# Keeping one piece of w3 in its slot between two layers of a decode kernel, with one slot fewer for wq

## The chip, the cores and the metric

The kernel runs on one core of one Trainium2 chip. The metric is device microseconds of one execution, median of three runs. The core has a tensor engine (PE, with its weight loads, PEld), a vector engine (DVE), a scalar engine (ACT), GpSimd (POOL), and a sync engine (SP) that here issues nearly all DMA transfers. All transfers from HBM go through one queue that 16 DMA engines serve, each with a fixed sixteenth of every transfer.

## The reference

One token (a vector of 640 values) goes through two identical layers with shared weights and shared caches. Cut to what matters:

```
W = 4096                                   # the last 4096 cached positions
q = (LN(x) @ wq) as 32 heads of 192        # wq: 640 x 6144
o = softmax(q k^T / sqrt(192)) v           # per head: k, v are 4096 x 192, bf16
x = x + o @ wo                             # wo: 6144 x 640
g = LN(x) @ w1 ; u = LN(x) @ w3            # w1, w3: 640 x 1536
x = x + (silu(g) * u) @ w2                 # w2: 1536 x 640
(the same four steps once more, same weights, same caches)
```

Keys, values and weights are the same in both layers, so what still lies in on-chip memory from layer 0 need not be read again in layer 1.

## The kernel before, in words

All large data lie in one on-chip buffer, `arena`, cut into 32 units ("slots") of 3072 bf16 columns on 128 partitions, 768 KB each. A page of k or v is 6144 columns, two slots. The list `loads` names every transfer of the program in the order of its issue: for each layer the pieces of wq, the pages of k and v, the pieces of wo, then w1, w3 and w2 (the kinds "fa", "fb", ...). `refill()` takes the head of that list, `place()` looks for free slots, and the transfer is issued on SP (L279; L268 for the fixed buffers `wo5` and `keep`); if no slot is free, the list stops there, strictly in order. `done(key)` is written behind the last matmul that reads a piece: it gives the slots back and calls `refill()`. So a transfer's issue on SP waits for the matmuls that read the slot's old contents, and SP's later transfers wait behind it. SP also keeps at most eight transfers under way, so where slots are plenty it issues one whenever the oldest has landed.

Some k heads of layer 0 stay for layer 1: 13 pages (26 slots) remain in the arena, a 14th is moved to PSUM and a spare buffer (`stash`, DVE copies on L288) and copied back in layer 1. At the end of layer 0 only slots 0, 1, 4 and 5 are therefore in turn for wo, w1, w3, w2 and, behind them, layer 1's wq.

Layer 0's FFN (`ffn`) reads w1 and w3 in pieces of one slot: fa and fb (w1, two of five row chunks each), fc (w1's last and w3's first chunk), fd (w3's chunks 1 and 2), fe (w3's chunks 3 and 4); fg and fh are w2, whose last 2240 columns stay in `keep` for both layers. A chunk is 1536 columns, and four matmuls on four column groups of PE compute it. Layer 1 loads w1 as one transfer (fa, 7680 columns), w3 as fb (4608) and fc (3072), and w2 in three parts under the key fd.

Between the layers (`attention`, `q_piece`), layer 1's wq comes as ten one-slot pieces, in the order q0, q12, q24, q36, q48 (first half of the heads), then q6, q18, q30, q42, q54. Six matmuls read each (1.04 us at the clock there); then its slot takes the next load. After the first five, ACT copies the result out and `q_turn` transposes it; q6 and q18 follow, then the first k page (head 8, still in the arena), and q30, q42 and q54 each behind one k page. Each retained k page that is read gives two slots. The first new loads behind wq are halves of k and v pages ("k", 1, 12, half 0), and so on.

At the end of layer 1, `ffn` runs its steps in program order: five chunks of w1 (`g_ps`), `out_residual` (two f32 matmuls that add the residual), then w3 (`u_ps`) with `gate()` (SiLU of g) behind the second w3 chunk, then ACT's copy of u (L588), `turn(1)`, the product on DVE (L590, `htd`), and `last_rows`: 48 matmuls with w2, 14 of them from `keep`. A DVE copy (L617) and a transfer of 1.2 KB (L619) end the kernel. PE's order is fixed by `pin`.

Of the kernel before, what the change touches and what calls it, by code (L numbers as in the profile page):

```python
# [17 lines left out]
NCH = 5  # L18
# [7 lines left out]
PGW = 6144  # L26
# [18 lines left out]
KEEP = 2240  # L45
# [10 lines left out]
def kernel(  # L56
# [39 lines left out]
    onesD, rl, st, nv, rstd, lnv, l = (sc[:, a:b] for a, b in ((0, 1), (1, 3), (3, 5), (7, 8), (5, 6), (6, 7), (6, 8)))  # L96
# [57 lines left out]
    loads = []  # L154
# [4 lines left out]
    w3_v = B_w3.rearrange("(p c) n -> p (c n)", c=NCH)  # L159
    w2_v = B_w2.rearrange("(p f) n -> p (f n)", f=12)  # L160
# [3 lines left out]
    def head(layer, g):  # L164
        return HG * ORDER[layer][g // HG] + g % HG

    def k_head(layer, g):
        return HG * ORDER[1][0] + (0, 1, 2, 3, 6, 4, 5, 7)[g] if layer == 1 and g < HG else head(layer, g)

    def k_first(layer, i):  # L170
        return layer == 0 and H - HB <= i < H
# [12 lines left out]
    def q_pieces(layer):  # L184
        if layer == 0:
            at = (0, 12, 24, 60)
            return [tuple(range(a, b)) for a, b in zip(at, at[1:])]
        return [tuple(range(12 * c + 6 * f, 12 * c + 6 * f + 6)) for f in range(2) for c in range(NCH)]
# [4 lines left out]
    def units_of(width):  # L193
        return -(-width // U)

    for layer in range(2):
        for piece in q_pieces(layer):
            n, at = 512 * len(piece), 512 * piece[0]
            loads.append((("q", layer, piece[0]), units_of(n), [(0, n, wq_r[:, at:at + n])]))
        for i in range(H + LEAD):  # L200
            kinds = (("v", i - LEAD, A_v_cache), ("k", i, A_k_cache))
            for kind, g, cache in kinds[::-1] if k_first(layer, i) else kinds:
                if not 0 <= g < H:
                    continue
                h = k_head(layer, g) if kind == "k" else head(layer, g)
                if kind == "k" and layer == 1 and h in RETAIN:
                    if h == STASH:
                        loads.append((("k", 1, h), 2, []))
                    continue
                src = cache[0, h, S0:SK, :].rearrange("(p t) d -> p (t d)", p=P)  # L210
                if layer == 1 and (kind, h) in SPLIT:
                    for th in range(2):
                        loads.append(((kind, layer, h, th), 1, [(0, U, src[:, U * th:U * th + U])]))
                else:
                    loads.append(((kind, layer, h), 2, [(0, PGW, src)]))
        for key, ranges in wo_units(layer):
            at, parts = 0, []
            for pos, lo, hi in ranges:
                parts.append((at, hi - lo, wo_v[ORDER[layer][pos]][:, lo:hi]))
                at += hi - lo  # L220
            if key:
                loads.append((key, units_of(at), parts))
            else:
                dst = wo5 if at == 2560 else wo4
                if dst is wo5:
                    src = parts[0][2]
                    parts = [(o, n, src[:, o:o + n]) for o, n in tail_cuts(2560)]
                loads.append((None, None if dst is wo5 else LAST, [(dst[:, o:o + n], src) for o, n, src in parts]))
        if layer == 0:
            loads.append((("fa", layer), 1, [(0, 3072, w1_v[:, 0:3072])]))  # L230
            loads.append((("fb", layer), 1, [(0, 3072, w1_v[:, 3072:6144])]))
            loads.append((("fc", layer), 1, [(0, 1536, w1_v[:, 6144:]), (1536, 1536, w3_v[:, 0:1536])]))
            loads.append((("fd", layer), 1, [(0, 3072, w3_v[:, 1536:4608])]))
            loads.append((("fe", layer), 1, [(0, 3072, w3_v[:, 4608:])]))
            loads.append((("fg", layer), 1, [(0, W2A, w2_v[:, 0:W2A])]))
            loads.append((("fh", layer), 1, [(0, 7680 - KEEP - W2A, w2_v[:, W2A:7680 - KEEP])]))
            loads.append((None, None, [(keep[:, o:o + n], w2_v[:, 7680 - KEEP + o:7680 - KEEP + o + n])
                                       for o, n in tail_cuts(KEEP)]))
        else:
            loads.append((("fa", layer), units_of(7680), [(0, 7680, w1_v[:, 0:7680])]))  # L240
            loads.append((("fb", layer), 2, [(0, 4608, w3_v[:, 0:4608])]))
            loads.append((("fc", layer), 1, [(0, 3072, w3_v[:, 4608:])]))
            loads.append((("fd", layer), 2, [(o, n, w2_v[:, o:o + n]) for o, n in ((0, 3200), (3200, 1280), (4480, 3200 - KEEP))]))

    def place(key, n):
        at = [s for s in free if all(s + i in free for i in range(n))]
# [44 lines left out]
    def page(key, width=PGW):  # L291
        return arena[:, home[key][0] * U:home[key][0] * U + width]
# [257 lines left out]
    def ffn(layer, last, spread):  # L550
        g_ps = ps_a.tile([P, 512], F32, tag="a", name="g_ps")
        u_ps = ps_a.tile([P, 512], F32, tag="a", name="u_ps")
        gu = w20.rearrange("p (g n) -> p g n", g=2)
        gt_ps = (m_ps[:, 0:12], g_ps[:, 384:396])

        def turn(gi):
            for k in range(3):
                mm(gt_ps[gi][:, 4 * k:4 * k + 4], lhsT=gu[:, gi, k:384:3], rhs=sel4, start=True, stop=True)

        def gate():  # L560
            pin(nc.scalar.mul(out=gu[:, 0, :], in_=g_ps[:, 0:384], mul=rstd))
            turn(0)
            pin(nc.scalar.activation(out=ex[:], in_=gt_ps[0], func=ACTF.Exp, scale=-1.0))
            pin(nc.vector.tensor_scalar_add(out=ex[:], in0=ex[:], scalar1=1.0))
            pin(nc.vector.reciprocal(out=ex[:], in_=ex[:]))
            pin(nc.vector.tensor_tensor(out=ut[:], in0=gt_ps[0], in1=ex[:], op=ALU.mult))

        if layer == 0:
            steps = ((g_ps, "fa", 0, 2, 0), (g_ps, "fb", 2, 4, 0), (g_ps, "fc", 4, 5, 0),
                     (u_ps, "fc", 0, 1, 1536), (u_ps, "fd", 1, 3, 0), (u_ps, "fe", 3, 5, 0))  # L570
        else:
            steps = ((g_ps, "fa", 0, 5, 0), (u_ps, "fb", 0, 3, 0), (u_ps, "fc", 3, 5, 0))
        for n, (ps, kind, c0, c1, off) in enumerate(steps):
            pg = page((kind, layer), 7680 if (kind, layer) == ("fa", 1) else PGW)
            for c in range(c0, c1):
                for j in range(4):
                    mm(ps[32 * j:32 * j + 32, 0:384], lhsT=xs[:, c, 3:35],
                       rhs=_ap(pg, 0, P, off + 1536 * (c - c0) + 3 * j, [[12, 128], [1, 3]]),
                       start=(c == 0), stop=(c == NCH - 1), tile_position=(0, 32 * j))
                if ps is g_ps and c == 0:  # L580
                    spread()
                if ps is u_ps and c == layer:
                    gate()
            if layer == 0 and all(st[1] != kind for st in steps[n + 1:]):
                done((kind, layer))
            if layer and n == 0:
                out_residual(*last)
        pin(nc.scalar.mul(out=gu[:, 1, :], in_=u_ps[:, 0:384], mul=rstd))  # L588
        turn(1)
        pin(nc.vector.tensor_tensor(out=_ap(htd[:], 0, P, 0, [[1, 3], [3, 4]]),  # L590
                                    in0=gt_ps[1].rearrange("p (k j) -> p k j", k=3),
                                    in1=ut[:].rearrange("p (k j) -> p k j", k=3), op=ALU.mult))
        if layer == 1:
            return last_rows(last[0])
        y_ps = y_open("y2_ps")
        for fcx in range(9):
            j = fcx % 4
            for nh in range(2):
                lo, hi = 640 * fcx + 320 * nh, 640 * fcx + 320 * nh + 320
                cuts = [lo] + [7680 - KEEP] * (lo < 7680 - KEEP < hi) + [hi]  # L600
                for c0, c1 in zip(cuts, cuts[1:]):
                    mm(y_ps[nh][32 * j:32 * j + 1, c0 - lo:c1 - lo], lhsT=htd[:, fcx:fcx + 1], rhs=w2_cols(layer, c0, c1 - c0),
                       start=False, stop=(fcx >= 5 and c1 == hi), tile_position=(0, 32 * j))
            if 640 * fcx < W2A <= 640 * fcx + 640:
                done(("fg", layer))
        done(("fh", layer))
        y_to_residual(y_ps, (keep[:, KEEP - TAIL:], htd, 9))
# [107 lines left out]
```

## Time and profile before

| | |
|---|---|
| runs | 524.82, 525.02, 525.16 us; median 525.02 |
| profiled execution | 524.09 us, of which its instructions span 522.3 us |
| moved from HBM | 219.78 MB, 421 GB/s over the span |
| busy | PE 290.0 us (56%), DVE 261.6 (50%), ACT 81.3 (16%), POOL 22.3 (4%) |
| chain that ended last | DMA 85%, PE 9%, DVE 3%, ACT 1% |

The digit rows of the page cut the span into 40 slices: the DMA row is 9 (90% or more) in every slice but the last. PE and DVE are busy half of the time. A timeline row gives start and duration, the engine and line, the operation with its operands and count, and in brackets the idle time before it with what ended it.

### The profile page before, as it was taken

The numbers are of one execution on the slowest core, as the hardware profiler recorded it, in microseconds if no ns is written. First come the engines' busy times: TensorE is split into PE (matmuls) and PEld (weight loads), VectorE is DVE, ScalarE is ACT, GpSimd is POOL, SyncE is SP. The second block draws the span as 40 slices with busy tenths as digits, with TensorE's granted clock in tenths as the row PEclk, the third lists the DMA queues.
The fourth block names the chain that finished last, engine by engine and source line by source line (L and its number), as shares of the span: only waits on it lengthen the run. The fifth ranks groups of instructions, "written<-read, shape, count | busy, mean of one in ns | idle before, by whom it ended". The sixth has DMA issues, their size and how long they took to land.

```text
span 522.3 us, 5553 instructions
## 1 busy us (share of the span) xinstructions
PE 290.0 (56%) x2163; PEld 107.7 (21%) x2163; DVE 261.6 (50%) x338; ACT 81.3 (16%) x224; POOL 22.3 (4%) x104
## 2 busy tenths in 40 slices
PE   3325755364555645556466786677346655364565
PEld 1101221121212112112112232222112212121132
DVE  0079876556746576763001107532678565565111
ACT  1010211120303021112001013122301220122001
POOL 4010000000000000000000001000000000000100
PEclk9677677777776668666666567889557787778667
DMA  9999999999999999999999999999999999999996
GB/s 377 404 429 431 430 428 429 427 429 429 433 427 432 429 428 431 427 430 429 424 416 415 423 404 427 429 429 429 429 429 432 428 429 429 428 431 427 433 429 263
DMA packets 24081, 220.13 MB, mean 421 GB/s; under 512 B 2808, under 2 KB 3704, under 8 KB 8952
## 3 DMA queue, kind: packets, MB, share of 16 engines
q1 hardware_dynamic: 23912, 219.79, 99.5%
q8 instruction: 17, 0.28, 0.2%
q14 instruction: 8, 0.07, 0.0%
q10 hardware_dynamic: 144, 0.00, 0.0%
HBM read 219.78 MB, written 0.00 MB: 421 GB/s over the span
## 4 chain that ended last, share of the span: by engine, by line
DMA 85%; PE 9%; DVE 3%; ACT 1%; issue 1%; SPq 0%; ACTq 0%; DVEq 0%
DMA arena<-in_A_k_cache_dram 47%; DMA arena<-in_A_v_cache_dram 28%; DMA arena<-in_B_w_dram 5%; PE s_ps L87 4%; DMA arena<-in_A_wo_dram 3%; DMA arena<-in_A_wq_dram 3%; PE o_ps L87 2%; DVE arena L397 2%; PE pss L87 1%; PE q_ps L87 1%; PE y_ps L87 1%; ACT w L472 0%; DVE w L472 0%; SPq L279 0%; ACT ptm L444 0%
## 5 line engine op out<-in xcount | busy, mean ns | idle before, releaser
L87 PE MATMUL s_ps<-arena,wst 128*16 128x512 bf16 (+1 forms) x768 | 143.6, 523 | 146.0 <-DVE arena L397 69.9
L397 DVE STREAM_TRANSPOSE arena<-arena 128x3072 uint32<-128x3072 uint32 (+1 forms) x53 | 168.5, 3189 | 58.6 <-DMA arena<-in_A_k_cache_dram 58.2
L87 PE MATMUL o_ps<-arena,ptm 128*16 128x512 bf16 (+1 forms) x768 | 130.2, 495 | 20.5 <-DMA arena<-in_A_v_cache_dram 20.5
L87 PEld LDWEIGHTS <-wst 128*16 128x16 bf16 (+1 forms) x768 | 46.7, 109 | 233.4 <-issue 208.9
L87 PEld LDWEIGHTS <-ptm 128*16 128x16 bf16 (+1 forms) x776 | 37.9, 105 | 73.4 <-issue 58.3
L428 ACT ACTIVATE lt<-w 32x16 f32<-32x16 f32 x16 | 3.4, 211 | 263.3 <-DVE w L425 263.3
L444 ACT COPY ptm<-w 32x96 bf16<-32x96 bf16 x80 | 25.9, 324 | 48.4 <-PE o_ps L87 34.4
L472 DVE CAST w<-o_ps 32x512 bf16<-32x512 f32 x16 | 11.0, 689 | 40.5 <-ACT w L472 40.3
L87 PE MATMUL q_ps<-arena,xs 128*32 128x512 bf16 x120 | 19.5, 587 | 13.9 <-DMA arena<-in_A_wq_dram 12.8
L87 PE MATMUL pss<-w,sel 96*64 96x192 bf16 x64 | 12.2, 278 | 23.1 <-ACT w L472 15.3
L420 DVE TENSOR_REDUCE lt<-s_ps 64x1 f32<-64x512 f32 x16 | 10.9, 684 | 24.6 <-PE s_ps L87 22.6
L472 ACT CAST w<-o_ps 32x512 bf16<-32x512 f32 x32 | 18.4, 575 | 25.9 <-PE o_ps L87 25.4
L382 POOL COPY wst<-qt_sb 32x24 bf16<-32x24 bf16 x30 | 8.4, 280 | 323.3 <-PE s_ps L87 241.2
L434 DVE STREAM_TRANSPOSE w<-w 64x512 bf16<-64x512 bf16 x16 | 11.3, 705 | 14.7 <-ACT w L431 13.8
L87 PE MATMUL y_ps<-arena,otd 128*1 128x320 bf16 x176 | 14.0, 420 | 7.6 <-DMA arena<-in_A_wo_dram 7.3
L444 DVE COPY ptm<-w 32x96 bf16<-32x96 bf16 x48 | 10.8, 226 | 10.5 <-PE o_ps L87 9.4
L87 PEld LDWEIGHTS <-xs 128*32 128x32 bf16 x200 | 7.6, 111 | 30.3 <-issue 25.8
L382 DVE COPY wst<-qt_sb 32x24 bf16<-32x24 bf16 x4 | 0.8, 212 | 25.8 <-ACT qt_sb L369 25.8
L327 DVE CAST w<-y_ps 128x320 bf16<-128x320 f32 x3 | 1.5, 492 | 23.7 <-PE y_ps L87 23.7
L87 PEld LDWEIGHTS <-sel 96*64 96x64 bf16 x64 | 6.1, 118 | 30.9 <-ACT w L472 16.7
L431 ACT ACTIVATE w<-s_ps,eu 64x512 bf16<-64x512 f32 x16 | 10.9, 682 | 6.0 <-DVE eu L429 6.0
L478 DVE SCALAR_TENSOR_TENSOR w<-pss,sc,cb 64x192 bf16<-64x192 f32 x16 | 6.6, 410 | 9.1 <-PE pss L87 9.1
(86 smaller groups left out, 126.6 us busy)
## 6 DMA issues: line engine op xcount, KB each, us to landing
arena<-in_A_v_cache_dram SPq DMA_DIRECT2D x62, 1536.0 KB, 29.2
arena<-in_A_k_cache_dram SPq DMA_DIRECT2D x47, 1536.0 KB, 29.2
arena<-in_A_wq_dram SPq DMA_DIRECT2D x10, 768.0 KB, 7.4
arena<-in_A_wq_dram SPq DMA_DIRECT2D x1, 4608.0 KB, 19.8
arena<-in_A_k_cache_dram SPq DMA_DIRECT2D x6, 768.0 KB, 9.7
arena<-in_A_wo_dram SPq DMA_DIRECT2D x6, 720.0 KB, 7.8
arena<-in_B_w_dram SPq DMA_DIRECT2D x5, 768.0 KB, 7.7
arena<-in_A_wo_dram SPq DMA_DIRECT2D x2, 1920.0 KB, 30.1
```

The lines of the kernel that those rows point to most:

```text
L87: return pin(nc.tensor.matmul(*a, **k))
L327: pin(nc.vector.tensor_copy(out=y_sb[:, 320:640], in_=y_ps[1][:, 0:320]))
L382: pin((engs[a].copy if engs[a] is nc.scalar else engs[a].tensor_copy)(out=dst, in_=src))
L397: pin(nc.vector.transpose(x.bitcast(U32), x.bitcast(U32)))
L420: pin(nc.vector.reduce_max(out=t0[:, 0:1], in_=s_ps[0:64, :], axis=AX.X))
L428: pin(nc.scalar.mul(out=t0[32:64, 0:KW].rearrange("p (a z) -> p a z", a=4), in_=mb, mul=-SCALE))
L431: pin(nc.scalar.activation(out=e[:], in_=s_ps[0:64, :], func=ACTF.Exp, bias=nbt[:, 0:1], scale=SCALE, accum_out=l[0:64, b % 2:b % 2 + 1]))
L434: pin(nc.vector.transpose(et[:], e[:]))
L444: pin((eng.copy if eng is nc.scalar else eng.tensor_copy)(out=dst, in_=src))
L472: pin(nc.vector.tensor_copy(out=dst, in_=src) if c == 2 else nc.scalar.copy(out=dst, in_=src))
L478: pin(nc.vector.scalar_tensor_tensor(out=om, in0=ot_ps, scalar=rl[0:64, b % 2:b % 2 + 1], in1=mask[0:64].unsqueeze(2).broadcast_to([64, 16 ...
```

## The change

Layer 0's fe (w3's columns 4608 to 7680, the row chunks 3 and 4) is not given back after its use: its slot, number 0, stays occupied until the end. Layer 1 reads those two chunks from it, directly behind w1, and loads only the rest of w3, as 3072 columns (fb) and 1536 columns (fc). The key fc of layer 1 shrinks to half, the three w2 transfers are cut at 3200, 4800 instead of 3200, 4480. The gate comes behind chunk 4, which is now the second one in the order. Start and stop flags of the accumulation follow the new order of chunks. With slot 0 gone, three slots (1, 4 and 5) are in turn for wq between the layers.

```diff
-            loads.append((("fb", layer), 2, [(0, 4608, w3_v[:, 0:4608])]))
-            loads.append((("fc", layer), 1, [(0, 3072, w3_v[:, 4608:])]))
-            loads.append((("fd", layer), 2, [(o, n, w2_v[:, o:o + n]) for o, n in ((0, 3200), (3200, 1280), (4480, 3200 - KEEP))]))
+            loads.append((("fb", layer), 1, [(0, 3072, w3_v[:, 0:3072])]))
+            loads.append((("fc", layer), 1, [(0, 1536, w3_v[:, 3072:4608])]))
+            loads.append((("fd", layer), 2, [(o, n, w2_v[:, o:o + n]) for o, n in ((0, 3200), (3200, 1600), (4800, 2880 - KEEP))]))
...
-            steps = ((g_ps, "fa", 0, 5, 0), (u_ps, "fb", 0, 3, 0), (u_ps, "fc", 3, 5, 0))
+            steps = ((g_ps, "fa", 0, 5, 0), (u_ps, "fe", 3, 5, 0), (u_ps, "fb", 0, 2, 0), (u_ps, "fc", 2, 3, 0))
         for n, (ps, kind, c0, c1, off) in enumerate(steps):
-            pg = page((kind, layer), 7680 if (kind, layer) == ("fa", 1) else PGW)
+            pg = page((kind, 0 if kind == "fe" else layer), 7680 if (kind, layer) == ("fa", 1) else PGW)
+            edge = [st for st in steps if st[0] is ps]
...
-                       start=(c == 0), stop=(c == NCH - 1), tile_position=(0, 32 * j))
+                       start=(c == edge[0][2]), stop=(c == edge[-1][3] - 1), tile_position=(0, 32 * j))
...
-                if ps is u_ps and c == layer:
+                if ps is u_ps and c == 4 * layer:
                     gate()
-            if layer == 0 and all(st[1] != kind for st in steps[n + 1:]):
+            if layer == 0 and kind != "fe" and all(st[1] != kind for st in steps[n + 1:]):
                 done((kind, layer))
```

## The prediction

> **What bounds the kernel now.** I read the page first: transfers by slice, then queues.
>
> ```profile
> DMA  9999999999999999999999999999999999999996
> GB/s 377 404 429 431 430 428 429 427 429 429 433 427 432 429 428 431 427 430 429 424 416 415 423 404 427 429 429 429 429 429 432 428 429 429 428 431 427 433 429 263
> q1 hardware_dynamic: 23912, 219.79, 99.5%
> ```
>
> The one queue is full in all slices but the last, at some 429 GB/s. Bytes taken out should therefore be time taken out, unless the queue runs dry elsewhere, or something other than the queue sets the end. Both have to be looked at: the stretch between the layers, where four slots carry wq (three after the change), and the tail, where the bytes are saved. First the stretch, the issues on SP (one answer for each narrow window) and PE's rows on the pieces of wq:
>
> ```profile
> 286.01 0.33 SPq L279 DMA_DIRECT2D arena<-in_A_wq_dram  x1
> 288.52 0.33 SPq L279 DMA_DIRECT2D arena<-in_A_wq_dram  x1
> 289.17 0.33 SPq L279 DMA_DIRECT2D arena<-in_A_wq_dram  x1
> 293.29 0.33 SPq L279 DMA_DIRECT2D arena<-in_A_wq_dram  x1
> ```
> ```profile
> 292.22 1.04 PE L87 MATMUL q_ps<-arena,xs 128*32 128x512 bf16 x6 [0.53 <-DVE xs L313]
> ...
> 295.38 1.04 PE L87 MATMUL q_ps<-arena,xs 128*32 128x512 bf16 x6 [0.63 <-DMA arena<-in_A_wq_dram]
> ...
> 297.22 1.04 PE L87 MATMUL q_ps<-arena,xs 128*32 128x512 bf16 x6 [0.80 <-DMA arena<-in_A_wq_dram]
> ...
> 299.10 1.04 PE L87 MATMUL q_ps<-arena,xs 128*32 128x512 bf16 x6 [0.85 <-DMA arena<-in_A_wq_dram]
> ...
> 302.11 1.04 PE L87 MATMUL q_ps<-arena,xs 128*32 128x512 bf16 x6 [0.86 <-DMA arena<-in_A_wq_dram]
> ...
> 303.94 1.04 PE L87 MATMUL q_ps<-arena,xs 128*32 128x512 bf16 x6 [0.79 <-DMA arena<-in_A_wq_dram]
> ```
>
> PE starts a piece 0.04 us after it lands and frees its slot 1.04 us later; pieces land 1.85 us apart. The queue runs only as far ahead as slots are free. Where this lead was shortest, behind the last pieces, the rate is already down:
>
> ```profile
> 300.00:304.00 4.00, 1.51 (x16) 0.53 (x16) 0.42 (x2) 2.00 (x6) 1.10 (x4) 0.50 1.02 422
> 304.00:308.00 4.00, 4.00 (x24) 1.53 (x25) 0.00 (x0) 0.00 (x0) 0.00 (x0) 0.50 1.01 395
> 308.00:312.00 4.00, 4.00 (x36) 1.81 (x34) 0.00 (x0) 0.00 (x0) 0.00 (x0) 0.84 1.00 389
> ```
>
> (Last column GB/s, the one before it the DMA share.) Then the tail:
>
> ```profile
> 511.17 0.52 PE L87 MATMUL g_ps<-arena,xs 128*32 128x384 bf16 x4 [1.75 <-DMA arena<-in_B_w_dram]
> ...
> 513.63 0.76 PE L87 MATMUL pss<-arena 128*128 128x160 f32 x2
> ...
> 514.32 0.87 PE L87 MATMUL u_ps<-arena,xs 128*32 128x384 bf16 x8
> ...
> 515.29 1.25 PE L87 MATMUL u_ps<-arena,xs 128*32 128x384 bf16 x12
> ...
> 517.74 0.44 PE L87 MATMUL pss<-keep,htd 128*1 128x160 bf16 x14 [0.28 <-DVE htd L590]
> 517.96 0.76 PE L87 MATMUL pss<-arena,htd 128*1 128x160 bf16 x28
> 519.01 0.30 PE L87 MATMUL pss<-arena,htd 128*1 128x160 bf16 x6 [0.29 <-DMA arena<-in_B_w_dram]
> ```
>
> Once w1 has landed (PE waits for it, the first row) no PE row names a transfer until the very last six matmuls. From 511.17 to 517.74 PE, ACT and DVE are the chain, not the queue; the w3 pieces, 513.79 and 515.62 in the trace's completion records, come just in time.
>
> **The change, part by part.**
>
> *The bytes saved.* 3072 columns on 128 partitions are 786 KB, one piece, 1.85 us of queue. But they stand in the queue behind w1, so w1's landing does not move for it. The chain behind w1 keeps its work: 20 matmuls of g, the f32 pair, 20 of u, gate behind the second u chunk in both versions, ACT, turn, DVE; the eight matmuls on the kept slot stand behind g in PE's order, so they fill no idle time before w1. At most 0.05 us go (515.66, when the fourth u chunk started, against 515.61 by spacing). So `htd` comes as before, 6.7 us behind w1. What can go is the wait at the end: 48 matmuls start in groups of four 0.069 us apart, so with all of w2 there the last starts at 517.75 + 11 x 0.069 = 518.51 and ends 0.23 later, 518.74, instead of 519.31. The w2 parts would land by 518.97 - 1.85 = 517.1, so they are there. Gain 0.57 us, not 1.85.
>
> *Smaller cuts, the same number of transfers (six) on SP.* Hidden while the queue is full: SP issues them 20 to 32 us ahead of landing. Without that cover, 0.33 us each.
>
> *One slot fewer in layer 1.* Followed through `place` and `done`, every page of k and v takes the slots of a later release, one page later. In the trace pages from 346 us on are issued up to 24 us after their slots came free, 29 us before they land; the nearest release then, the first wo piece, moves from 460.3 to 472.9 for a transfer that starts at 493. Cost 0. The stashed page's seven DVE copies (3.4 us) move from behind v's to behind k's release, some 10 us later, on a DVE that is half idle; the pages queued behind them have their slots over 20 us early: 0. The POOL work of `out_open` falls into the last v page's slot in both: 0.
>
> *Three slots for wq.* The piece that went out at 286.01 into fe's slot now takes the one of 288.52; each later piece one release later:
> - third piece 289.17, lands 295.34 as before;
> - fourth: waits for PE to finish the first, 293.26, and goes out at 293.29, where it used to go at 289.17 and land at 297.18.
>
> The trace has no 768 KB transfer that went out with nothing ahead of it, so what a short lead costs is bounded from rows. The three with the least lead were issued at 303.19, 305.01 and 307.54; of their 16 engines the first reported 3.9 us after the issue, those not held up by the transfer before some 4.3, the last of those 4.7. The shortest complete one (279.71, w3's last) took 5.3. Lower bound 3.9: 293.29 + 3.9 = 297.19, no loss. Upper bound 5.3: 298.6, a loss of 1.4. I take 4.5, between the two and next to the 4.3: lands 297.8, loss 0.6 us. Then:
> - fifth: goes out 294.79, lands 299.65; sixth: 296.45, 301.5, on one engine 1.4 us later (it was so held up before, where this piece landed 3.0 us after its predecessor: a 16 KB instruction fetch at 298.79 lies there);
> - ninth: waits for the sixth's matmuls, 302.9 + 0.04 + 1.04 = 304.0; lands not before 308.5, in the flow it would be 307.05: 15 engines lose up to 1.4, the late one (308.4) nothing;
> - first half of a k page: waits for the first retained page, whose matmuls ended 2.56 us after the seventh piece's (307.54 against 304.98). Seventh now done at 305.8, so 308.4 + 4.5 = 312.9; late engine in the flow 312.2: loss 0.7.
>
> The second half lands at 314.8, where it landed at 313.63: +1.15 us on the last engine, +2.5 on the mean engine (before, the records spread from 311.43 to 313.63, the mean at 312.0). Behind it slots are plentiful (issues 4 to 10 us ahead and growing), the queue stays full, and the delay is carried to w1's landing. Before, one engine alone was late and the others were up to 2 us ahead; the seven instruction fetches between 320 and 505 us, each setting an engine back some 1.2 to 1.5 us, were absorbed in that lead. After, all stand level, so the last engine at w1 is between 1.15 (none counts) and 2.6 (1.15 + 1.45) late. I take 2.2, since seven of 16 engines are hit.
>
> **Sum** against the profiled execution (524.09, 522.3 span and 1.8 around it; the median is 0.93 above it): 2.2 - 0.57 = +1.6. On the median 525.02: 526.6. The profile's span should be 523.9 in an execution like the one shown.
>
> The Trainium skill, "DMA: Bandwidth & Descriptors", section "Anatomy of one DMA", gives a transfer a fixed part of some 2.0 us plus bytes / 436 GB/s (fitted on transfers that GpSimd issues); worked out from it, an estimate, 768 KB take 3.8 us alone, and three slots would carry the stream without a gap. By it the sum would be -0.57 alone, 524.45. The trace's 3.9 for the first engine is close to it; its 4.3 to 4.7 for the others is not.
>
> **Rivals.**
> 1. *No gap (the other side).* If a piece with no lead lands whole within 3.9 us of its issue, the fourth lands at 297.19 and nothing later is late: 524.4. For it: the issues at 294.79 and 296.45 in before cost nothing at a lead of 2.7 us and more. Against: 395 and 389 GB/s at 304 to 312. It decides at 3.9 us.
> 2. *The bytes count.* PE works faster than I read, and w2's landing sets the end: 525.02 - 1.85 = 523.2. Against it: no row of the tail waits for a transfer.
> 3. *Gaps, but the late engine is all:* the others catch up under it: +1.15 - 0.57: 525.6.
> 4. *Worse:* 5.3 us for a piece; the fourth costs 1.4 instead of 0.6, the ninth and the k half 0.4 more each: 2.2 + 1.6 - 0.57 = +3.2: 528.2.
>
> **How the numbers follow.** My forecast (526.1 to 527.3) has 0.55, rival 4 0.15, rival 3 0.13, rival 1 0.12, rival 2 0.05. Change under 0.2% (1.05 us) is about what cannot be told from none. Faster by more: rival 2, 0.05. Within: rivals 1 and 3, 0.25. Slower: 0.70. The range 525.0 to 527.9 leaves out rival 2, two thirds of rival 1 and half of rival 4, 0.2 in all.
>
> **What would show it.** In the stretch: the fourth wq piece issued at 293.3 and its matmuls not before 297.7; a row under 415 GB/s between 294 and 300 and again at 304 to 312; fewer slices at 429. In the tail: w1's wait ending some 2 us later, no PE row behind it waiting for a transfer, the last w2 matmuls in one run behind `htd`, and 6.7 us from w1 to `htd`. I am wrong if PE's fourth piece starts at 297.2, if w1 lands where it did, or if `htd` comes earlier behind w1.

## The result, and the profile after

| | before | after |
|---|---|---|
| median of six runs (range), us | 524.71 (524.42 to 525.16) | 528.11 (526.82 to 529.28) |
| ratio to before, 95% interval | | 1.0061 (1.0044 to 1.0077) |
| profiled execution, span, us | 524.09, 522.3 | 528.06, 526.3 |
| read from HBM, MB | 219.78 | 218.99 |

The changed kernel reads 0.79 MB less and is 3.4 us slower, 0.65%. The forecast had the sign and half of the size: 526.6, with 527.9 as the upper end.

The page of the changed kernel, transfers by slice:

```profile
DMA  9999999999999999999999999999999999999995
GB/s 374 405 430 429 429 429 428 431 429 430 428 429 431 427 429 430 430 431 430 415 419 415 336 349 425 432 431 427 426 431 432 430 423 430 432 432 424 432 428 223
```

Two slices, 289 to 316 us, fall to 336 and 349 GB/s, where before had 423 and 404. Every other slice but the last is within 9 GB/s of before. The same stretch of the changed kernel in windows of 4 us (last column GB/s, the one before it the DMA share):

```profile
288.00:292.00 4.00, 3.31 (x42) 1.86 (x41) 0.82 (x3) 0.43 (x1) 0.00 (x0) 0.50 0.98 383
292.00:296.00 4.00, 2.89 (x16) 1.21 (x16) 0.78 (x4) 0.41 (x2) 0.00 (x0) 0.50 0.96 347
296.00:300.00 4.00, 1.15 (x10) 0.39 (x11) 0.00 (x0) 0.00 (x0) 0.00 (x0) 0.50 0.80 280
300.00:304.00 4.00, 2.23 (x16) 0.48 (x11) 0.00 (x0) 0.76 (x2) 0.00 (x0) 0.50 0.94 360
304.00:308.00 4.00, 1.85 (x12) 0.58 (x14) 0.42 (x2) 1.24 (x5) 1.11 (x4) 0.50 0.92 336
308.00:312.00 4.00, 4.00 (x31) 1.66 (x29) 0.00 (x0) 0.00 (x0) 0.00 (x0) 0.66 1.05 370
312.00:316.00 4.00, 4.00 (x42) 1.82 (x36) 0.00 (x0) 0.69 (x1) 0.00 (x0) 1.00 0.91 358
```

The mean is 348 GB/s. Of the same seven windows of before, the prediction shows three (422, 395 and 389 GB/s); the other four are:

```profile
288.00:292.00 4.00, 2.99 (x37) 1.82 (x32) 1.06 (x5) 0.42 (x1) 0.00 (x0) 0.50 1.04 429
292.00:296.00 4.00, 3.16 (x20) 1.19 (x21) 0.54 (x3) 0.41 (x2) 0.00 (x0) 0.50 1.01 424
296.00:300.00 4.00, 2.35 (x14) 0.40 (x11) 0.00 (x0) 0.00 (x0) 0.00 (x0) 0.50 1.02 423
312.00:316.00 4.00, 1.99 (x22) 0.82 (x16) 1.80 (x7) 1.92 (x6) 0.76 (x3) 1.00 1.01 422
```

The mean of before is 415. 67 GB/s over 28 us are 1.9 MB not moved, at 429 GB/s 4.4 us. The DMA share falls less, to 0.80 in one row and 0.91 or more in the others: a packet that waits counts as busy (a packet of 6144 bytes takes 0.23 us in the full flow, and up to 1.4 us in this stretch), so the rate shows the loss and the share hides most of it.

PE's rows on the fourth to seventh wq piece, and SP's issue of the fourth:

```profile
293.89 0.33 SPq L279 DMA_DIRECT2D arena<-in_A_wq_dram  x1
```
```profile
299.89 1.04 PE L87 MATMUL q_ps<-arena,xs 128*32 128x512 bf16 x6 [2.48 <-DMA arena<-in_A_wq_dram]
301.75 1.04 PE L87 MATMUL q_ps<-arena,xs 128*32 128x512 bf16 x6 [0.82 <-DMA arena<-in_A_wq_dram]
...
304.67 1.04 PE L87 MATMUL q_ps<-arena,xs 128*32 128x512 bf16 x6 [0.78 <-DMA arena<-in_A_wq_dram]
...
307.19 1.04 PE L87 MATMUL q_ps<-arena,xs 128*32 128x512 bf16 x6 [1.48 <-DMA arena<-in_A_wq_dram]
```

The fourth piece is used at 299.89, 6.0 us after its issue; in before it was used at 297.22, and the forecast had 297.8. The tail of the changed kernel:

```profile
515.59 0.53 PE L87 MATMUL g_ps<-arena,xs 128*32 128x384 bf16 x4 [1.76 <-DMA arena<-in_B_w_dram]
...
518.90 0.87 PE L87 MATMUL u_ps<-arena,xs 128*32 128x384 bf16 x8
...
519.87 1.22 PE L87 MATMUL u_ps<-arena,xs 128*32 128x384 bf16 x12
...
522.30 0.44 PE L87 MATMUL pss<-keep,htd 128*1 128x160 bf16 x14 [0.28 <-DVE htd L591]
522.51 0.79 PE L87 MATMUL pss<-arena,htd 128*1 128x160 bf16 x34
```

w1 lands at 515.46 (511.04 in before), 4.4 us later. From there to the first w2 matmul it is 6.84 us (6.70), and all 34 matmuls on loaded w2 columns run in one piece, no longer waiting for a transfer. So 4.4 us are lost between the layers, and 0.4 gained at the end.

### The profile page after: what moved, and what is told of

Same layout as the page of the kernel before. It is cut to its first block, busy times and chain, and to the rows that moved or that the text cites. A ratio compares the mean times of both kernels' runs of the same rounds, so it can differ in the third digit from the quotient of the medians.

```text
span 526.3 us, 5542 instructions
## 1 busy us (share of the span) xinstructions
PE 289.2 (55%) x2163; PEld 107.6 (20%) x2163; DVE 261.6 (50%) x338; ACT 81.3 (15%) x224; POOL 22.4 (4%) x104
## 3 DMA queue, kind: packets, MB, share of 16 engines
HBM read 218.99 MB, written 0.00 MB: 416 GB/s over the span
## 4 chain that ended last, share of the span: by engine, by line
DMA 84%; PE 9%; DVE 3%; ACT 2%; issue 1%; SPq 1%; DVEq 0%; ACTq 0%
DMA arena<-in_A_k_cache_dram 41%; DMA arena<-in_A_v_cache_dram 30%; DMA arena<-in_B_w_dram 7%; PE s_ps L87 3%; DMA arena<-in_A_wo_dram 3%; DMA arena<-in_A_wq_dram 2%; PE o_ps L87 2%; DVE arena L397 2%; PE pss L87 1%; PE q_ps L87 1%; PE y_ps L87 1%; PE g_ps L87 1%; PE u_ps L87 1%; SPq L279 1%; ACT ptm L444 0%
## 5 line engine op out<-in xcount | busy, mean ns | idle before, releaser
L87 PE MATMUL s_ps<-arena,wst 128*16 128x512 bf16 (+1 forms) x768 | 141.0, 514 | 145.8 <-ACT wst L382 74.1
L87 PE MATMUL o_ps<-arena,ptm 128*16 128x512 bf16 (+1 forms) x768 | 133.7, 505 | 18.8 <-DMA arena<-in_A_v_cache_dram 18.8
L87 PE MATMUL y_ps<-arena,otd 128*1 128x320 bf16 x176 | 12.8, 383 | 8.8 <-DMA arena<-in_A_wo_dram 8.4
L382 DVE COPY wst<-qt_sb 32x24 bf16<-32x24 bf16 x4 | 0.8, 212 | 28.3 <-ACT qt_sb L369 28.2
## 6 DMA issues: line engine op xcount, KB each, us to landing
arena<-in_A_v_cache_dram SPq DMA_DIRECT2D x62, 1536.0 KB, 29.2
arena<-in_A_k_cache_dram SPq DMA_DIRECT2D x47, 1536.0 KB, 29.2
arena<-in_A_wo_dram SPq DMA_DIRECT2D x2, 1920.0 KB, 24.8
```

The source lines that it names most:

```text
L87: return pin(nc.tensor.matmul(*a, **k))
L382: pin((engs[a].copy if engs[a] is nc.scalar else engs[a].tensor_copy)(out=dst, in_=src))
```

## Experiments

Each kernel is compared with runs of the kernel before on its own chip (medians 524.80, 524.38 and 524.56 in the three sets).

**The bytes without the slot's loss.** From the changed kernel:

```diff
-            pg = page((kind, 0 if kind == "fe" else layer), 7680 if (kind, layer) == ("fa", 1) else PGW)
+            pg = wo4 if layer and kind == "fe" else page((kind, layer), 7680 if (kind, layer) == ("fa", 1) else PGW)
...
-            if layer == 0 and kind != "fe" and all(st[1] != kind for st in steps[n + 1:]):
+            if layer == 0 and all(st[1] != kind for st in steps[n + 1:]):
```

> The bytes are saved as in the change, but the slot goes back after layer 0 and four slots carry wq; layer 1 reads its two w3 chunks from other data that is there anyway (wo's kept columns), so its output leaves out the right values of these two chunks. My theory: the loss of the change is all in the three slots, and PE's chain behind w1 lets only 0.4 to 0.6 us of the saved 1.85 us through: before minus 0.5 us, w1 landing where it did in before. Rival, the bytes count: before minus 1.85 us.

Measured: 524.30 us against 524.80, ratio 0.9986 (0.9971 to 1.0001). The stretch is nearly back (420 and 385 GB/s in the two slices). The end, from w1's landing to the last instruction, takes 10.82 us instead of 11.27:

```profile
513.01 0.52 PE L87 MATMUL g_ps<-arena,xs 128*32 128x384 bf16 x4 [1.04 <-DMA arena<-in_B_w_dram]
...
519.69 0.44 PE L87 MATMUL pss<-keep,htd 128*1 128x160 bf16 x14 [0.28 <-DVE htd L591]
519.90 0.79 PE L87 MATMUL pss<-arena,htd 128*1 128x160 bf16 x34
```

0.45 of 1.85 us come through, as forecast. w1's landing itself came 1.8 us later than in the one execution of before: half of that is the mean of the 16 DMA engines, half the spread (the last engine was 2.0 us behind the mean here, 1.1 in before). The two kernels below that load the same bytes through four slots have it at 510.9 and 511.1, so this is one execution's scatter.

**The slot's loss without the bytes.** From the kernel before:

```diff
-            if layer == 0 and all(st[1] != kind for st in steps[n + 1:]):
+            if layer == 0 and kind != "fe" and all(st[1] != kind for st in steps[n + 1:]):
```

> All bytes are loaded as in before, only layer 0's slot of fe is not given back until the end. My theory: before plus 3.8 to 4.0 us (the change's 3.4 and the 0.4 to 0.5 that its tail gains), all of it between 288 and 316 us and in what the instruction fetches add behind it. Rival, the slower time comes from the new cuts or the new order of chunks: before within 1 us.

Measured: 528.83 against 524.80, +4.0 us, ratio 1.0076 (1.0057 to 1.0095). With the -0.5 of the first kernel that makes +3.5; the change has +3.4. Within the intervals the two parts add up, and the new cuts cost nothing that shows.

**The same only while wq is read.** The slot comes back behind the last wq piece (`done(("fe", 0))` after `q_copy` in `attention`).

> The kernel before with fe's slot withheld only while wq is read; it comes back behind the last wq piece. My theory: the loss arises in the stretch alone, so this is as slow as with the slot withheld to the end, before plus 3.5 to 4.3 us. Rival, part of the loss is the smaller arena in the rest of layer 1: clearly less, plus 2 us or under.

Measured: 529.12 against 524.38, +4.7 us, ratio 1.0090 (1.0071 to 1.0108), more than the 3.5 to 4.3 expected. The interval overlaps that of the kernel before this one; the rival, that the smaller arena costs in the rest of the layer, is out.

**Lone pieces.** One slot for wq: fe, fg and fh are withheld and come back behind the last wq piece, so that seven pieces go out behind an empty queue.

```diff
-                done(("fg", layer))
+                pass
...
-        done(("fh", layer))
...
                 if not late:
                     q_copy(q_ps)
+                    done(("fe", 0), ("fg", 0), ("fh", 0))
```

> The kernel before with three slots withheld, so that one carries wq and each of six pieces goes out alone, behind an empty queue: the disputed cost by itself, read from issue to landing. The prediction's 4.5 us would give a piece every 5.6 us and before plus 26 us; 5.2 us gives plus 31, 6.0 plus 36. If lone pieces take 4.3 to 4.5 us, the 6.0 of the changed kernel's fourth piece needs another cause than the missing lead.

Measured: 549.50 against 524.38, +25.1 us, ratio 1.0475 (1.0456 to 1.0494). Issue to landing of the pieces issued at 293.21 and 303.72 (an instruction fetch falls into the second), then at 315.19 and 325.73, one answer of the trace each:

```profile
DMA to landing us min/median/max: 4.2/4.2/4.2
DMA to landing us min/median/max: 5.1/5.1/5.1
DMA to landing us min/median/max: 4.1/4.1/4.1
DMA to landing us min/median/max: 4.3/4.3/4.3
```

A lone 768 KB piece takes 4.1 to 4.3 us on its last engine; on the first, by the completion records (one for each of the 16 engines and each transfer), 3.6 to 3.8. A lead is in what follows the time from a piece's issue to an engine's report of the piece before: below zero for these lone pieces, mostly 3 us and more in the flow of before. The prediction's 4.5 was not too small as the price of a missing lead. The 6.0 of the changed kernel's fourth piece needs another cause, as the expectation said.

**Two slots.** fe and fg withheld in the same way.

> The kernel before with two slots (fe's and fg's) withheld while wq is read, so that two carry it: a cycle of two pieces is the time from issue to the last engine's report plus 1.1 us of PE and issue. If a piece without lead takes 4.4 us (the prediction's size) that is 2.75 us a piece, 0.9 more than the flow's 1.85, over six to seven pieces: before plus 6 us. If it takes 5.2 us: plus 9. If 6.0, as the fourth piece of the changed kernel did: plus 12.

Measured: 535.60 against 524.38, +11.2 us, ratio 1.0210 (1.0191 to 1.0230). PE's rows on the second to seventh piece:

```profile
293.87 1.04 PE L87 MATMUL q_ps<-arena,xs 128*32 128x512 bf16 x6 [0.58 <-DMA arena<-in_A_wq_dram]
297.05 1.04 PE L87 MATMUL q_ps<-arena,xs 128*32 128x512 bf16 x6 [2.13 <-DMA arena<-in_A_wq_dram]
300.13 1.04 PE L87 MATMUL q_ps<-arena,xs 128*32 128x512 bf16 x6 [2.04 <-DMA arena<-in_A_wq_dram]
303.74 1.04 PE L87 MATMUL q_ps<-arena,xs 128*32 128x512 bf16 x6 [2.57 <-DMA arena<-in_A_wq_dram]
307.29 1.04 PE L87 MATMUL q_ps<-arena,xs 128*32 128x512 bf16 x6 [1.41 <-DMA arena<-in_A_wq_dram]
310.90 1.04 PE L87 MATMUL q_ps<-arena,xs 128*32 128x512 bf16 x6 [2.57 <-DMA arena<-in_A_wq_dram]
```

A piece every 3.1 us, from the fourth of these on every 3.6. The whole is near the +12 expected for 6.0 us a piece, but only one engine needs that long. The pieces issued at 301.20, 304.81, 308.37 and 311.97 land after 6.0, 6.1, 5.9 and 6.0 us. In the completion records 15 of the 16 engines report each of these pieces 3.6 to 4.2 us after its issue, as if it were alone, and one reports 1.7 to 2.0 us behind them, piece after piece. That engine got late around the instruction fetch at 298.8 us (16 KB). From then on each new piece is issued 2.3 to 2.5 us before that engine reports the old one, and the engine pays 1.6 to 1.9 us more than its 1.85 us of work each time. The packet records show how: the piece of 301.20 was out, the engine's old work ended at 303.42, and its first new packet begins at 304.40 and takes 0.96 us instead of 0.23; for the next piece the engine stands idle from 306.98 to 308.20. It starts late: idle for 1.0 and 1.2 us with the next piece already issued, about as long as from an issue to the first packet on the other engines (0.95 us). In the one-slot kernel an engine that got late at a fetch (at 303.7) was level again with the next piece, because the queue was empty when that piece was issued.

**The fourth piece later.** The first wq piece's slot is given back only with the second's.

```diff
-        done(("q", layer, piece[0]))
+        if layer == 0 or piece[0] > 12:
+            done(("q", layer, piece[0]))
+        elif piece[0] == 12:
+            done(("q", layer, 0), ("q", layer, 12))
```

> The changed kernel with the first wq piece's slot given back only with the second's, so that the fourth piece goes out some 1.6 us later (295.5 instead of 293.9), when the engines are nearly out of work, and the fifth right behind it. If a short lead just costs the time from issue to landing (the prediction's way to count), all is 1.6 us later: 529.7. If the extra is paid by engines that are still busy for about 2 us at the issue, the fourth piece lands 4.2 us after it, at 299.7 as before, the fifth 1.85 later, and the time is the changed kernel's within 0.7 us or less.

Measured: 528.91 against 524.56, ratio 1.0074 (1.0055 to 1.0093), so +4.4 us where the change has +3.4. The fourth piece is issued at 295.02, 1.1 us later than in the changed kernel, and it is used no later (PE's rows on the third to fifth piece):

```profile
295.79 1.04 PE L87 MATMUL q_ps<-arena,xs 128*32 128x512 bf16 x6 [0.79 <-DMA arena<-in_A_wq_dram]
299.54 1.04 PE L87 MATMUL q_ps<-arena,xs 128*32 128x512 bf16 x6 [2.71 <-DMA arena<-in_A_wq_dram]
302.94 1.04 PE L87 MATMUL q_ps<-arena,xs 128*32 128x512 bf16 x6 [2.36 <-DMA arena<-in_A_wq_dram]
```

299.54 against 299.89: for PE, which waits for the last engine, the earlier issue brought nothing. The mean engine did land the fourth piece earlier in the changed kernel, at 298.14 against 299.08, but at the fifth piece the two are level, 301.10 and 301.03: the fifth piece, issued here 3.4 to 4.1 us before the engines reported the fourth, followed it within 1.9 us on 15 of them, where with leads of mostly 2.1 to 2.6 us in the changed kernel it took 2.97 on the mean. For these two pieces the second reading is right. For the whole time the run decides less: +1.0 us over the change lies between the two expectations, the fifth piece caught a late engine (302.9), and the eighth and ninth piece then went out with leads under 1 us on most engines and lost 1.3 and 1.8 us on the mean, as lone pieces do.

**Two queues.** In the changed kernel the fifth, seventh and ninth wq piece and the first half k page are issued from ACT.

```diff
+            other = key in (("q", 1, 48), ("q", 1, 18), ("q", 1, 42), ("k", 1, 12, 0))
...
-                pin(nc.sync.dma_start(out=arena[:, s * U + off:s * U + off + w], in_=src))
+                pin((nc.scalar if other else nc.sync).dma_start(out=arena[:, s * U + off:s * U + off + w], in_=src))
```

> The changed kernel with every second piece of the short-lead stretch (the fifth, seventh, ninth of wq and the first half k page) issued from ACT's queue instead of SP's. The lone piece took 4.1 to 4.3 us, a piece issued while an engine still works on the one before up to 6: if that extra belongs to the order within one queue, each queue now starts empty, the extra goes, and the time is the changed kernel's minus 1 to 2 us. If it belongs to the engines, whichever queue feeds them: the changed kernel within 0.7 us.

Measured: 529.13 against 524.56, ratio 1.0076 (1.0055 to 1.0098), no gain over the change; +4.6 us where the change has +3.4, above the 0.7 us that was allowed, with intervals that overlap. The fifth piece, alone in its queue, still landed 7.4 us after its issue, and the mean engine reported it 2.99 us behind the fourth, 1.1 more than its work (1.12 in the changed kernel). The extra does not belong to the order within one queue.

**The tail.** In the changed kernel the kept chunks go ahead of w1, and with them the residual, which follows the first step:

```diff
-            steps = ((g_ps, "fa", 0, 5, 0), (u_ps, "fe", 3, 5, 0), (u_ps, "fb", 0, 2, 0), (u_ps, "fc", 2, 3, 0))
+            steps = ((u_ps, "fe", 3, 5, 0), (g_ps, "fa", 0, 5, 0), (u_ps, "fb", 0, 2, 0), (u_ps, "fc", 2, 3, 0))
...
-                if ps is u_ps and c == 4 * layer:
+                if ps is u_ps and c == layer:
```

> The changed kernel with the kept chunks' eight matmuls and the residual's pair ahead of w1's, in PE's idle time before w1 lands; the gate comes behind the second loaded chunk. My theory (PE's chain behind w1 is the bound of the tail): 1.7 us less PE work behind w1, so that w2's landing becomes the bound and 1.3 us of them are gained: the changed kernel minus 1.3 us, 526.8. Rival, the tail is bound by the transfers already: no gain.

Measured: 528.39 against 524.80, ratio 1.0060 (1.0041 to 1.0080): no gain that shows over the change's 1.0061, a miss. The trace says why:

```profile
515.98 0.88 PE L87 MATMUL u_ps<-arena,xs 128*32 128x384 bf16 x8 [0.53 <-DVE xs L313]
516.79 0.90 PE L87 MATMUL pss<-arena 128*128 128x160 f32 x2
517.62 0.53 PE L87 MATMUL g_ps<-arena,xs 128*32 128x384 bf16 x4
```

w1 landed at 516.30, but its matmuls start at 517.62: the normalized vector came only at 515.93, and the moved work fills 1.6 us of PE, of which only some 0.3 lies in idle time. From w1's landing to the first w2 matmul it is 6.53 us instead of 6.84. The same order on the bytes alone:

> The first kernel of this set (bytes alone, four slots, two chunks' values left out) with PE's order of the third. My theory: now the whole 1.85 us of the saved transfer come through, before minus 1.8 us, w2's last matmuls waiting for their transfer again. Rival, something else than PE's chain holds the tail: as the first kernel, before minus 0.5.

Measured: 523.71 against 524.80, ratio 0.9984 (0.9973 to 0.9996); 10.46 us from w1's landing to the end. Also less than expected, for the same reason: w1 landed at 510.87, its matmuls start at 512.13. Last, only the residual's pair moved, out of the loop to ahead of it:

> The kernel with the bytes alone, with only the residual's f32 pair moved ahead of w1's landing (0.8 us of PE, which fits the idle time there; the eight matmuls and the pair together took 1.6 us and made w1's matmuls late). Two w3 chunks' values are left out as there. PE's chain as the bound: the bytes-alone kernel minus 0.6 us, before minus 1.1, with w2's last part landing as PE comes to it. Transfers as the bound: no gain over the bytes-alone kernel.

Measured: 523.78 against 524.38, ratio 0.9987 (0.9977 to 0.9998). In the trace the end is as expected: w2's matmuls start 6.0 us behind w1's landing, and it is 10.02 us to the last instruction, 0.8 us less than with the bytes alone. Between the medians of the two kernels only 0.1 us is left of that, within their intervals; by the clock it stays undecided.

**All executions side by side**, from the completion records: mean over the 16 engines from the first wq piece to the fourteenth piece of this stretch, from there to w1 of layer 1, and from w1's last landing to the end of the span (us).

| kernel | stretch | rest to w1 | w1 to end |
|---|---|---|---|
| before | 24.8 | 194.1 | 11.27 |
| bytes alone | 25.6 | 194.2 | 10.82 |
| the same, kept chunks first | 24.8 | 194.2 | 10.46 |
| the same, residual first | 24.8 | 194.1 | 10.02 |
| changed kernel | 29.2 | 194.1 | 10.83 |
| slot alone | 28.2 | 194.1 | 11.15 |
| slot alone, in the stretch | 30.1 | 194.1 | 11.25 |
| changed, kept chunks first | 30.0 | 194.1 | 10.53 |
| changed, two queues | 29.0 | 194.1 | 10.66 |
| changed, fourth piece later | 30.3 | 194.1 | 10.76 |
| two slots | 35.0 | 194.1 | 11.26 |
| one slot | 50.7 | 194.1 | 11.27 |

What the mean engine loses in the stretch arrives in full, and nothing is added or made up behind it in 194 us. The three-slot kernels are 3.4 to 5.6 us behind before there.

## Why the prediction was right and wrong

*The bytes saved: right.* -0.57 forecast; -0.44 in the changed kernel's trace (10.83 against 11.27), -0.45 with the bytes alone, which by the medians are -0.5 us, with an interval that just includes no change. PE's chain behind w1 holds the tail: its length to `htd` stays (6.84 for 6.70), no PE row behind w1 waits for a transfer, and taking work out of that chain shortened it (6.0 with the residual ahead). Rival 2, -1.85 us, is out, by these runs and not by the reason given there: the last row of the tail that the prediction shows does wait for a transfer.

*The smaller arena and the cuts, cost 0: right.* 194.1 us behind the stretch in every kernel, and as slow with the slot back after wq.

*Three slots for wq: right in place and direction, too small by half.* The stretch is where it was named, and 304 to 312 us is again low. The loss begins earlier than forecast: the second piece, issued at 289.09 where the forecast has 288.52, already costs the mean engine 0.45 us (0.1 to 0.4 in the other three-slot executions). The failed term is the +2.2 us of delay at w1: it is 4.4.

The step that failed is the price of a lead that is short but not gone. The forecast let a piece land either 4.5 us after its issue or 1.85 us behind the piece before, whichever is later, so a piece that is issued some 2 to 3 us before the engines report the one before cost nothing. With an empty queue the figure is 4.1 to 4.3, and 4.5 was not too small. But the fourth piece had 13 engines within 4.3 us of the issue, and three at 4.7 to 6.0. PE needs all 16, so the slot's next load, the seventh, went out at 300.96 where the forecast's steps give 298.9, and the fifth, to which the forecast gave no loss of its own, cost the mean engine 1.12 us.

By pieces, the mean engine lost in the changed kernel 0.45 (second), 0.95 (fourth), 1.12 (fifth), 0.22, 0.62, 0.40 (sixth to eighth), 0.25, 0.35 (ninth, tenth) and 0.74 (half k page): 5.1 us, where before lost 0.7. The forecast had losses at the fourth, ninth and k piece only, 2.5 us on the mean. The completion records divide the 5.1: if each engine reported a piece 3.9 us after the issue or 1.85 us behind the one before, whichever is later, the issues of the changed kernel would cost 2.2 us, near the forecast's 2.5. The other 2.9 (0.7 in before), 1.1 of them at the fifth piece, come on top, and the forecast had no term for them; where the packet records were followed, they are late starts.

The forecast also carried the delay by the last engine: +1.15 us there, turned into 2.2 at w1 by later instruction fetches. In these two executions the last engine was 3.3 us late behind the second half k page (316.92 against 313.62) and 4.4 at w1, so the 1.05 added for the fetches came out at 1.1; what was too small is the 1.15. The mean is still the safer term: it is 4.4 already at the fourteenth piece, and the time from there to w1 is the same in all twelve kernels, while the last engine's differs by 1.4 us.

Rival 4 had the number (528.2) by a price of 5.3 us for each piece without lead. That price is not what the runs show for a lone piece, so its number is luck. Rival 1 (no gap) and rival 3 (only the late engine counts) are out. The rule of the Trainium skill that stood beside rival 1 ("DMA: Bandwidth & Descriptors", "Anatomy of one DMA"), 2.0 us plus bytes by 436 GB/s for transfers that GpSimd issues, an estimate of 3.8 us for 768 KB, agrees with the first engine of a lone piece (3.6 to 3.8) and is 0.3 to 0.5 short for the last. What came on top, about half of the loss, is not in that sum.

What stays open is why an engine that is still busy for some 2 us when its next work is issued starts that work late. The runs show that it does, on either queue, and that it does hardly or not for a lead of 3 us or more or with an empty queue. They also show that the engines then stand idle: in the changed kernel, from 297.7 to 298.4 us, only 6 to 8 of the 16 had a packet in work, more than 2 us after the fifth piece was issued, and 15 again at 299.1. What holds them up inside is not visible in the traces.

## What to carry to other kernels

A slot that is kept to spare a transfer pays the transfer's bytes only if nothing but the queue bounds the place where they are saved, and it costs wherever the same slots hold the queue's lead: compare the two places before counting bytes. Where slots carry a stream of such pieces, ask that each transfer be issued at least 3 us before the engines report the one before, as here; count what is lost below that by the mean over the engines, and the wait of the reader by the last engine. In a queue that was full behind the stretch, as here, such a loss was not made up.

## What the runs showed of the hardware

Over all pieces of 768 KB of this stretch, in eleven executions (all kernels but the one with two queues), sorted by the time from the issue to the engine's landing of the piece before (engines matched by their order of landing): up to 1.5 us, an engine reports the new piece 3.9 us after the issue, whatever it was doing; from 3 us on it follows in 1.85 us (on the mean 0.2 us more between 3.0 and 3.2, under 0.1 beyond); between, at 2.4 to 2.7 us, it takes 5.0 on the mean, and in a tenth of the cases 5.8 or more, where 4.4 would be its work. A late engine can so stay late: 1.7 to 2.0 us behind for four pieces in a row with two slots, level again at once with one. The issue 1.1 us earlier of the same piece brought its reader nothing (299.89 against 299.54).

A queue that is full shows a constant time on the mean engine: 194.1 to 194.2 us for the same bytes in all twelve kernels, although the last engine's time for them differed by 1.4 us (193.4 to 194.8).
